# Scores and products with V side by side in two PSUM tiles, and batch 1's loads in the rooms of late weights

## The chip, the cores and the metric

The kernel runs on one NeuronCore of a Trainium2 chip. The metric is the device time of one execution in microseconds (us). Below, TensorE is PE in the profile's rows, VectorE DVE, ScalarE ACT, GpSimd POOL and SyncE SP; PEld is TensorE's loading of weights beside its matmuls.

## The reference, cut to what matters

```
scores = scale * q @ k.T                       # 4 batches, 8 heads, 576 positions, 64 wide
heads 0-3: causal, the last 32 positions       # "local"
heads 4-7: causal, same position modulo 32     # "strided"
attn = exp(scores - max) / (sum + 1e-9);  x = attn @ v            # -> 2304 tokens x 512
h = relu(x @ w_in);  x = (s*h*h + b) @ w_out                      # 512 -> 2048 -> 512
# then: 8 experts; a token goes on if x @ w_skip > 0, to its best expert by x @ w_gate
out = x;  out[sel] = x + gate * (relu(x @ w1[e]) @ w2[e])         # 512 -> 1024 -> 512
```

All of it is float32. Attention is computed only where the masks leave something.

## The kernel before, in words

The work of a token passes through three parts: attention, a dense layer of 2048 hidden units (called MoE below, as in the code), and the experts.

**Attention.** There are 16 pairs of heads, four for each batch, in the order local, strided, local, strided (`HPS`); pair n has batch n // 4. Each pair has three units (`add_unit`, line 313), so there are twelve units for each batch. A unit computes scores by matmuls (line 341) into the PSUM tile `sc`, the maximum over each row on VectorE (L349), exponentials with their sums on ScalarE (L359), the reciprocal and the product with it on VectorE (L368), a transposition on TensorE into the PSUM tile `pt` (L373), a copy to SBUF (`moved`, L377, recorded at L234), the product with V on TensorE into the PSUM tile `xo` (L390), and two copies into the MoE's input `xb`: a rounded part (L395, recorded at L234 or L236) and the rest by a subtraction on VectorE (L397). In pairs 0 to 7 the mask is added by a matmul (L336), and ScalarE reads the scores from PSUM; in later pairs VectorE adds the mask (L345) and so reads `sc` once.

**MoE.** The tokens are in six blocks of 384. For each block and each of 16 slices of 128 hidden units there is a stage: twelve matmuls (L1028) with a slice of `w_in`, activation on ScalarE and VectorE, nine matmuls (L1071) with a slice of `w_out`. `SEGS` orders the stages: block 0 with slices 0 to 7, block 1 with all, block 0 with the rest, then blocks 2 to 5. Stage 8 is thus the first of block 1, whose tokens belong to batches 0 and 1, and stage 16 is the first that wants slice 8 of the weights. Each slice of a weight comes as 64-bit numbers by DMA (L481) and is converted on ScalarE and VectorE (L488 to L504). The first eight stages begin with three dummy matmuls each (L1024), and batch 0's units with four (L334).

**The order of the work.** All tasks are given to a planner (`Plan`, line 71), with estimated durations, a priority (the lower goes first), predecessors and rooms. It goes through the time, always gives the ready task with the best priority to a free engine, and writes down the order; the engines then work through it in that order, each on its own queue, and wait for each other by semaphores that the framework sets. A room (`Buf`) is a tag of a tile: a task that takes it waits until the last user of one of its tags is done. `sc`, `pt` and `xo` are one PSUM tile each, a bank of 512 columns; batch 0 may also use `h` for scores and the three `x2p` for `pt` and `xo`, since the MoE doesn't need them yet. A unit's priority is `FIRST[b] + STEP[b] * k`, k being its place in the batch; its tasks on TensorE come before every MoE stage (-5000), those on the other engines compete with the conversion of weights, whose priority is the number of the stage. Units of batches 2 and 3 also wait for the stage that has their priority's number (`gates`, line 1166).

**Loads.** SyncE issues them in the planner's order. V of batch 0's four pairs has a room for each pair, in the tiles `wi8` to `wi11` and `wo8` to `wo11` that weights fill later (`V_ROOM`, line 254); V of all later pairs has the one tile `vl`, and its load waits for the pair before to finish its products (L307). Queries and keys lie in `qkl` (local) and `qks` (strided), one tile each, refilled after the scores of the pair that used it last (L303); those of pairs 0, 2 and 3 have rooms in the tiles of late weights (`QK_ROOM`, line 255).

**Routing.** After a block's last stage its rows are turned, and the logits of the gate are gathered over some 20 us in the tile `sc` (`add_routing`, line 545, L599).

Of the kernel before, what the change touches and what calls it, by code (L numbers as in the profile page):

```python
# [20 lines left out]
BLK = 384  # L21
# [12 lines left out]
FIRST = (-1000.0, 0.0, 26.0, 48.0)  # L34
STEP = (1.2, 0.6, 1.8, 1.3)
LATE, LEAD = 3.0, 0
# [15 lines left out]
CLS = [3 * t for t in range(10)] + [29]  # L52
NOWHERE = 4096

CAPS = {"s_": 2, "gh": 2, "gl": 2, "row": 3, "sm": 4, "h": 2}
# [98 lines left out]
def kernel(  # L154
# [49 lines left out]
    xb = [wp.tile([128, 2, 4, BLK], F32R, name=f"xb{i}") for i in range(3)]  # L204

    plan = Plan(CAPS)
    pools = {"s_": sp, "pts": sp, "r": sp, "sm": sp, "gh": gp, "gl": gp, "row": rp, "lo": rp, "h": ph, "sc": pm, "pt": pm, "xo": pm}

    def make(b, shape, dt):
        tag = b.tag  # L210
        pool = pools.get(tag) or (px if tag.startswith("x2p") else wp)
        return pool.tile(shape, dt, name=tag, bufs=CAPS.get(tag, 1))
# [8 lines left out]
    def c_a(n, psum=False):  # L221
        return {"A": (0.13 if psum else 0.16) + n / 1400}
# [4 lines left out]
    def c_dma(n):  # L227
        return {"SP": max(0.06, n / 360e3)}
# [24 lines left out]

    V_ROOM = {n: (f"wi{8 + n}", f"wo{8 + n}") for n in range(4)}
    QK_ROOM = {0: ("wi12", "wo12"), 2: ("wi13", "wo13"), 3: ("wi14", "wo7")}

    def add_pair(n):
# [22 lines left out]
        def load_v(e):  # L280
            if b == 0:
                for h in range(2):
                    vt[h] = make(vbuf[h], [nk, nt_all, D], F32)
                    SY.dma_start(vt[h][:], vd[:, h])
            else:
                v = vb[0:nk, 0:2 * nt_all * D].rearrange("p (h t d) -> p h t d", h=2, t=nt_all)
                SY.dma_start(v, vd)
                vt[:] = [v[:, 0], v[:, 1]]
# [12 lines left out]
        else:  # L301
            last = last_qk.get(loc)
            lq = [plan.add(c_dma(512 * src.shape[1]), load_qk, p0 - 4, after=s_tasks[last] if last is not None else (), lat=DMA)] * 2  # L303
            last_qk[loc] = n
        if b == 0:
            vbuf = [Buf([r]) for r in V_ROOM[n]]
        lv = plan.add(c_dma(4 * nk * 2 * nt_all * D), load_v, p0 - 3.5, after=o_tasks.get(n - 1, ()) if b else (), take=vbuf, lat=DMA)  # L307
        s_tasks[n], o_tasks[n] = [], []
# [4 lines left out]
    def add_unit(n, b, hp, g, loc, qk, vt, vbuf, qbuf, nq, nk, by_pe, prio, lq, lv):  # L313
# [3 lines left out]
        first = b == 0  # L317
        sc_b = Buf(["sc", "h"] if first else ["sc"])
        s_b = Buf(["s_", "gh"] if first else ["s_"])
        pt_b = Buf(["pt", "x2p0"] if first else ["pt"])  # L320
        pts_b = Buf(["pts", "gl"] if first else ["pts"])
        xo_b = Buf(["xo", "x2p1", "x2p2"] if first else ["xo"])
        sm_b = Buf(["sm"])
# [7 lines left out]
        def scores(e):  # L331
            d["sc"] = sc = make(sc_b, [128, 512], F32)
            for _ in range(KEEP_S if first else 0):
                PE.matmul(sc[:, 288:512], one, msk[:, 0:224], start=True, stop=True)  # L334
            if by_pe:
# [209 lines left out]
    def add_routing(blk, last, xbuf, paused=None, near=None):  # L545
        P = -8000 + blk
        d = rt[blk] = {"rows": {}, "lg": sp.tile([128, 3, 9], F32, name="lg")}
        lp_b, ls_b, lt_b = Buf(["sc"]), Buf(["lo"]), Buf(["pt"])
        row_b = [Buf(["row"]) for t in range(3)]
# [29 lines left out]
        for k in range(4):  # L579
# [15 lines left out]
            def logit(e, k=k):  # L595
                if k == 0:
                    d["lp"] = make(lp_b, [128, 512], F32)
                for m, x in ((18, d["xh"]), (9, d["xl"]))[::-1 if k == 3 else 1]:
                    PE.matmul(d["lp"][0:m, 0:BLK], wgr[:, k, 0:m], x[:], start=k == 0 and m == 18, stop=k == 3 and m == 18)  # L599

            a = plan.add(c_pe(128, 3, False), tr, P, after=cps + trs[:1], take=[pt_b] + ([] if trs else [lp_b]), use=row_b)
            trs.append(a)
            a = plan.add({**c_a(BLK, True), **c_v(BLK)}, xt_hi, P, after=[a], take=[hi_b], use=[pt_b])
            a = plan.add(c_v(BLK), xt_lo, P, after=[a], take=[lo_b], use=[pt_b, hi_b])
            lm = plan.add(c_pe(BLK, 2, False), logit, P, after=[a, lm, gate_w], use=[hi_b, lo_b, lp_b])

# [11 lines left out]

        a = plan.add({**c_a(BLK, True), **c_v(BLK)}, lg_row, P, after=[lm], take=[ls_b], use=[lp_b])
        a = plan.add({"PE": 0.35}, lg_turn, P, after=[a], take=[lt_b], use=[ls_b])  # L620
        lgs = [plan.add(c_v(54), lg_sum, P, after=[a], use=[lt_b])]
        sc_b = Buf(["sc"])
        a = plan.add({"V": 0.5}, lambda e: route_a(blk), P, after=lgs + [r_prev[0]])
# [161 lines left out]
    def turn():  # L785
        for t in range(4):
            if t < 3:
                pt = pm.tile([128, 4, 128], F32, name=("pt", "sc", "xo")[t])
            else:
                pt = ph.tile([128, 4, 128], F32, name="h")  # L790
            turn_in(pt, t)
            turn_hi(pt, t)
            turn_lo(pt, t)
# [62 lines left out]
    def last_x2(fill):  # L856
# [20 lines left out]
        for t in range(3):  # L877
            pt = pm.tile([128, 512], F32, name=("pt", "xo", "sc")[t])
            for k in range(4):
# [6 lines left out]
        ls = sp.tile([128, BLK], F32, name="r", bufs=1)  # L886
        lt = pm.tile([128, 512], F32, name="xo")
        for t in range(3):
# [14 lines left out]
    def experts():  # L903
# [17 lines left out]
        fill(3)  # L921
        rk, cn = (pm.tile([128, 512], F32, name=n_) for n_ in ("sc", "xo"))
        route_rank(NBLK - 1, rk)
# [172 lines left out]

    cn_b, ltp_b = Buf(["xo"]), Buf(["s_"])
    P, late = -7000, {}
# [161 lines left out]
```

## Time and profile before

| | us |
|---|---|
| three runs | 764.76, 763.86, 767.2 (median 764.76) |
| profiled execution | 763.24 |
| its span, first to last instruction | 761.4 |
| TensorE busy | 734.9 (97%) |
| VectorE busy | 375.4 (49%) |
| ScalarE busy | 296.0 (39%) |
| GpSimd busy | 62.7 (8%) |
| mean granted TensorE clock | 0.99 |

The profile is of one execution. Its times count from the first instruction. The page gives shares of the whole span; what belongs to one part of it is read from the views by stretch. A wait is put down to the engine that the semaphore came from last. A busy TensorE isn't TensorE at its peak, because matmuls overlap and their ends are modelled.

### The profile page before, as it was taken

How to read it: one execution, taken by the hardware profiler on the slowest of the kernel's cores; microseconds unless marked ns; L12 is line 12 of the kernel's file. 1: busy time of each engine (PE TensorE's matmuls, PEld its weight loads, DVE VectorE, ACT ScalarE, POOL GpSimd, SP SyncE). 2: the span in 40 equal slices, each digit the busy share in tenths (PEclk: the TensorE clock that was granted, in tenths of full speed). 3: DMA queues.
4: the chain of work that ended last, by engine and by line, in shares of the span. 5: the costliest groups of instructions: out<-in, count | busy, mean ns of one | idle time of the engine just before them, and what ended most of it. 6: DMA issues, size and time to landing. Idle time of an engine off the chain costs nothing.

```text
span 761.4 us, 11904 instructions
## 1 busy us (share of the span) xinstructions
PE 734.9 (97%) x4410; PEld 633.1 (83%) x4411; DVE 375.4 (49%) x1009; ACT 296.0 (39%) x813; POOL 62.7 (8%) x67
## 2 busy tenths in 40 slices
PE   9899989999999999999999999999999999999992
PEld 6788779998888888888888999898787888888791
DVE  4899999624565644456554324654442222313120
ACT  4787766424343543445453223533301402112020
POOL 0000000000010100010001002010032212011121
PEclk9999999999999999999999999999999999999997
DMA  9676685102231222012020005320214502011130
GB/s 294 221 208 207 201 280 142 51 0 84 76 113 48 71 65 80 27 48 78 27 84 1 2 1 174 107 80 5 79 36 142 220 37 75 14 42 56 43 72 32
DMA packets 23505, 69.00 MB, mean 91 GB/s; under 512 B 5035, under 2 KB 5291, under 8 KB 23430
## 3 DMA queue, kind: packets, MB, share of 16 engines
q1 hardware_dynamic: 19350, 56.81, 22.7%
q0 software_dynamic: 3936, 11.03, 4.7%
q8 instruction: 41, 0.67, 0.4%
q14 instruction: 34, 0.28, 0.1%
q10 hardware_dynamic: 144, 0.22, 0.1%
HBM read 52.94 MB, written 15.11 MB: 89 GB/s over the span
## 4 chain that ended last, share of the span: by engine, by line
PE 85%; DMA 5%; DVE 4%; issue 4%; ACT 1%; POOL 0%; POOLq 0%; DVEq 0%; ACTq 0%
PE h L1028 26%; PE x2p L1071 25%; PE h L801 10%; PE x2p L814 9%; DMA out<-row,ids 5%; PE sc L341 3%; PE xo L390 2%; PE pt L373 2%; PE sc L599 1%; PE pt L585 1%; PE h L1180 1%; PE h L341 1%; PE x2p L864 1%; PE h L1024 1%; DVE row L494 0%
## 5 line engine op out<-in xcount | busy, mean ns | idle before, releaser
L1028 PE MATMUL h<-xb,wi 128*128 128x384 f32 x1152 | 225.1, 344 | 2.0 <-ACT wi L234 1.2
L1028 PEld LDWEIGHTS h<-xb,wi 128*128 128x128 f32 x1152 | 203.9, 189 | 8.1 <-ACT wi L234 1.7
L1071 PE MATMUL x2p<-wo,gh 128*128 128x512 f32 x564 | 194.6, 399 | 0.0
L1071 PEld LDWEIGHTS x2p<-wo,gh 128*128 128x128 f32 x564 | 106.1, 188 | 20.1
L1071 PE MATMUL x2p<-wo,gl 128*128 128x512 f32 x282 | 111.1, 394 | 0.6 <-DVE gl L1061 0.4
L801 PE MATMUL h<-xb,wi 128*128 128x512 f32 (+1 forms) x480 | 103.3, 374 | 2.3 <-DVE row L818 1.8
L801 PEld LDWEIGHTS h<-xb,wi 128*128 128x128 f32 x480 | 83.4, 188 | 20.6 <-issue 2.8
L814 PE MATMUL x2p<-wi,wo 128*128 128x512 f32 x432 | 99.4, 390 | 0.0
L1036 DVE SCALAR_TENSOR_TENSOR r<-r,sbc 128x384 f32<-128x384 f32 x88 | 54.3, 617 | 85.7 <-ACT r L1033 85.6
L814 PEld LDWEIGHTS x2p<-wi,wo 128*128 128x128 f32 x432 | 80.8, 188 | 16.6
L1033 ACT ACTIVATE r<-h 128x384 f32<-128x384 f32 x96 | 47.0, 489 | 116.5 <-PE h L1028 111.2
L1040 ACT ACTIVATE gh<-r,sbc 128x384 fp32r<-128x384 f32 x88 | 54.3, 617 | 77.5 <-PE x2p L1071 53.6
L1045 DVE SCALAR_TENSOR_TENSOR gl<-r,sbc,gh 128x384 fp32r<-128x384 f32 x88 | 54.3, 617 | 59.1 <-ACT gh L1040 57.8
L804 ACT ACTIVATE wo<-h 128x512 fp32r<-128x512 f32 (+1 forms) x40 | 22.2, 554 | 144.0 <-PE h L801 139.1
L805 DVE SCALAR_TENSOR_TENSOR wo<-h,wo 128x512 fp32r<-128x512 f32 (+1 forms) x40 | 25.5, 638 | 76.5 <-ACT wo L804 72.3
L1071 PEld LDWEIGHTS x2p<-wo,gl 128*128 128x128 f32 x282 | 53.1, 188 | 9.4 <-DVE gl L1061 0.7
L703 POOL DMA_INDIRECT lst<-pay,ii x18 | 18.4, 1020 | 466.1 <-DVE ii L697 444.9
L818 DVE SCALAR_TENSOR_TENSOR row<-x2p,ids,xb 128x512 f32<-128x512 f32 x14 | 10.5, 751 | 61.8 <-PE x2p L814 61.8
L390 PEld LDWEIGHTS xo<-pts,vl 96*64 96x64 f32 (+1 forms) x480 | 16.9, 135 | 12.5 <-issue 4.5
L390 PE MATMUL xo<-pts,vl 96*64 96x64 f32 (+1 forms) x480 | 21.6, 226 | 3.6 <-DVE xb L397 2.1
L819 POOL DMA_INDIRECT out<-row,ids x14 | 13.9, 995 | 107.5 <-DVE row L818 93.2
L397 DVE TENSOR_TENSOR xb<-xo,xb 128x192 fp32r<-128x192 f32 (+4 forms) x59 | 18.3, 336 | 5.8 <-ACT xb L234 5.6
(479 smaller groups left out, 769.1 us busy)
## 6 DMA issues: line engine op xcount, KB each, us to landing
wo<-in_w SPq DMA_DIRECT2D x16, 512.0 KB, 5.8
qks<-in_qkstr SPq DMA_DIRECT2D x7, 882.0 KB, 6.5
wo<-in_w_out SPq DMA_DIRECT2D x12, 512.0 KB, 3.7
x2d<-row SPq DMA_DIRECT2D x21, 256.0 KB, 3.9
qkl<-in_qkloc SPq DMA_DIRECT2D x6, 864.0 KB
wo<-in_w_in SPq DMA_DIRECT2D x10, 512.0 KB, 4.0
out<-row SPq DMA_DIRECT2D x18, 256.0 KB, 2.0
wi<-in_w_in SPq DMA_DIRECT2D x6, 512.0 KB
```

The source lines that it names most:

```text
L341: PE.matmul(sc[0:nq, i * nk:(i + 1) * nk], qt, qk[0][:, k0:k0 + nk], start=not by_pe, stop=not by_pe or i == nt - 1)
L390: PE.matmul(xo[64 * h:64 * h + 64, c:c + m], vt[h][:, t, :], d["pts"][0:nk, r:r + m], start=True, stop=True)
L801: PE.matmul(p[:, 0:N], W[f][:, w, k * 128:(k + 1) * 128], x[:, k, 0:N], start=n == 0, stop=n == 11)
L804: A.activation(h[:, 0, 0:N], p[:, 0:N], AF.Relu)
L805: V.scalar_tensor_tensor(h[:, 1, 0:N], p[:, 0:N], 0.0, h[:, 0, 0:N].bitcast(F32), op0=ALU.max, op1=ALU.subtract)
L814: PE.matmul(y[:], K["h"][f][:, g, c], W[NFE + f][:, w, :], start=n == 0, stop=n == 3 * NFE - 1)
L1028: PE.matmul(p[:, 0:BLK], win_t[fc][:, w, k * 128:(k + 1) * 128], x[:, k, :], start=n == 0, stop=n == 11)
L1033: A.activation(d["r"][:], d["p"][:, 0:BLK], AF.Relu)
L1036: V.scalar_tensor_tensor(d["r"][:], d["r"][:], sbc[:, 0:1], d["r"][:], op0=ALU.mult, op1=ALU.mult)
L1040: A.activation(gh[:], d["r"][:], AF.Identity, bias=sbc[:, 1:2])
L1045: V.scalar_tensor_tensor(gl[:], d["r"][:], sbc[:, 1:2], gt[i][0][:].bitcast(F32), op0=ALU.add, op1=ALU.subtract)
L1071: PE.matmul(x2p[t][:], g[:, c], wout_t[fc][:, w, :], start=begins and n == 0, stop=ends and n == 2)
```

## The change

- The tiles `sc` and `xo` are replaced by two tiles `sx0` and `sx1` of one bank each. Of each, columns 0 to 287 are a room for scores (`sc0`, `sc1`) and columns 288 to 511 one for products with V (`xo0`, `xo1`). The number of PSUM banks stays at eight. A unit takes whichever score room and whichever product room the planner has free first.
- Routing takes `sc0` and `xo0` together for its logits, which are 384 columns wide.
- V of batch 1's four pairs gets the rooms `wi8` to `wi11` and `wo8` to `wo11` too, after batch 0's; its load no longer waits for the pair before.
- Queries and keys of pairs 6 and 7 get rooms in `wi12`, `wo12`, `wi13` and `wo13`, after those of pairs 0 and 2. `qkl` and `qks` then pass from pairs 4 and 5 to pairs 8 and 9.
- `STEP` of batch 1 goes from 0.6 to 0.3, so its units have priorities 0 to 3.3 instead of 0 to 6.6, and its loads come correspondingly earlier.
- The dummy matmuls of batch 0's units write columns 0 to 223 in place of 288 to 511.

```diff
-STEP = (1.2, 0.6, 1.8, 1.3)
+STEP = (1.2, 0.3, 1.8, 1.3)
...
+SCW = 288
...
+    sx = [pm.tile([128, 512], F32, name=f"sx{i}") for i in range(2)]
+    halves = {f"sc{i}": sx[i][:, 0:SCW] for i in range(2)} | {f"xo{i}": sx[i][:, SCW:512] for i in range(2)}
...
         tag = b.tag
+        if tag in halves:
+            return halves[tag]
...
-    V_ROOM = {n: (f"wi{8 + n}", f"wo{8 + n}") for n in range(4)}
-    QK_ROOM = {0: ("wi12", "wo12"), 2: ("wi13", "wo13"), 3: ("wi14", "wo7")}
+    V_ROOM = {n: (f"wi{8 + n % 4}", f"wo{8 + n % 4}") for n in range(8)}
+    QK_ROOM = {0: ("wi12", "wo12"), 2: ("wi13", "wo13"), 3: ("wi14", "wo7"), 6: ("wi12", "wo12"), 7: ("wi13", "wo13")}
...
         def load_v(e):
-            if b == 0:
+            if n in V_ROOM:
...
-        lv = plan.add(c_dma(4 * nk * 2 * nt_all * D), load_v, p0 - 3.5, after=o_tasks.get(n - 1, ()) if b else (), take=vbuf, lat=DMA)
+        lv = plan.add(c_dma(4 * nk * 2 * nt_all * D), load_v, p0 - 3.5, after=() if n in V_ROOM else o_tasks.get(n - 1, ()), take=vbuf, lat=DMA)
...
-        sc_b = Buf(["sc", "h"] if first else ["sc"])
+        sc_b = Buf(["sc0", "sc1"] + ["h"] * first)
...
-        xo_b = Buf(["xo", "x2p1", "x2p2"] if first else ["xo"])
+        xo_b = Buf(["xo0", "xo1"] + ["x2p1", "x2p2"] * first)
...
-                PE.matmul(sc[:, 288:512], one, msk[:, 0:224], start=True, stop=True)
+                PE.matmul(sc[:, 0:224], one, msk[:, 0:224], start=True, stop=True)
...
-        lp_b, ls_b, lt_b = Buf(["sc"]), Buf(["lo"]), Buf(["pt"])
+        lp_b, ls_b, lt_b = [Buf(["sc0"]), Buf(["xo0"])], Buf(["lo"]), Buf(["pt"])
...
-                    d["lp"] = make(lp_b, [128, 512], F32)
+                    d["lp"] = sx[0]
```

The rest of the diff passes the new names on (routing's other tasks, the count of tokens, and the experts' part, where the tiles are used whole).

## Rows read from the trace of the kernel before

**Rows 1.** The page, part 1: busy us of each engine (share of span), instructions.
```profile
PE 734.9 (97%) x4410; PEld 633.1 (83%) x4411; DVE 375.4 (49%) x1009; ACT 296.0 (39%) x813; POOL 62.7 (8%) x67
```

**Rows 2.** Table of stretches: length, busy us by engine (instructions), clock, DMA share, GB/s.
```profile
core 0: us, PE busy (x) PEld busy (x) DVE busy (x) ACT busy (x) POOL busy (x), PEclk, DMA share, GB/s
7.35:33.90 26.55, 25.92 (x342) 24.29 (x341) 20.08 (x89) 20.60 (x104) 0.00 (x0) 1.00 0.85 286
33.90:41.00 7.10, 5.12 (x22) 4.13 (x21) 7.10 (x22) 3.20 (x15) 0.00 (x0) 0.76 0.52 148
36.50:40.70 4.20, 3.41 (x12) 3.36 (x13) 4.20 (x13) 1.60 (x7) 0.00 (x0) 0.59 0.74 227
41.00:92.90 51.90, 50.92 (x397) 42.54 (x396) 48.53 (x129) 40.71 (x130) 0.00 (x0) 1.00 0.67 213
92.90:103.20 10.30, 6.02 (x73) 4.65 (x71) 10.23 (x29) 7.62 (x26) 0.00 (x0) 1.00 0.77 269
30.00:103.20 73.20, 65.47 (x550) 54.27 (x546) 69.33 (x192) 55.31 (x179) 0.00 (x0) 0.98 0.63 204
...
110.50:170.00 59.50, 59.50 (x299) 53.99 (x299) 39.93 (x72) 27.98 (x51) 0.00 (x0) 1.00 0.25 75
170.00:410.00 240.00, 239.78 (x1590) 210.30 (x1589) 126.82 (x396) 104.08 (x320) 9.31 (x9) 1.00 0.19 64
```

**Rows 3.** Waits, 92.9 to 103.3 us: who for whom, us, times, longest.
```profile
PE xo L390 <- DVE xb L397: 2.1, 1, 2.1
...
PE pt L373 <- DVE sm L352: 0.8, 1, 0.8
PE xo L390 <- ACT pts L234: 0.7, 1, 0.7
PE sc L336 <- ACT s__1369 L359: 0.7, 1, 0.7
```

**Rows 4.** Timeline of SyncE's queue: start, us, engine, line, transfer.
```profile
19.94 0.33 SPq L481 DMA_DIRECT2D wi<-in_w_in  x1
...
69.34 0.33 SPq L287 DMA_DIRECT2D vl<-in_vloc  x1
...
89.92 0.30 SPq L287 DMA_DIRECT2D vl<-in_vstr  x1
```

**Rows 5.** Chain of waits, 92.9 to 103.3 us: start, us, what.
```profile
93.58 0.60 DVE row L497
94.18 0.60 DVE row L494
...
99.76 0.60 DVE wi L504
100.36 0.60 DVE wo L504
100.96 0.34 DVE lo L491
```

**Rows 6.** Stretches, line 504 alone (last step of a conversion): VectorE's busy us, instructions.
```profile
30.00:103.20 73.20, 12.94 (x19) 0.98 0.63 204
```

**Rows 7.** Timeline of TensorE, 33 to 49 us: start, us, what, [idle before].
```profile
35.87 0.62 PE L1028 MATMUL h<-xb,wi 128*128 128x384 f32 x2 [1.18 <-ACT wi L234]
37.29 3.40 PE L1028 MATMUL h<-xb,wi 128*128 128x384 f32 x10 [0.80 <-DVE wi L504]
...
40.98 0.80 PE L341 MATMUL sc<-qkl 128*128 128x96 f32 x6
```

**Rows 8.** The page, part 6: loads of local queries and keys, KB each.
```profile
qkl<-in_qkloc SPq DMA_DIRECT2D x6, 864.0 KB
```

**Rows 9.** Timeline of VectorE, 100.9 to 102.6 us.
```profile
101.21 0.27 DVE L236 CAST xb<-xo 128x72 fp32r<-128x72 f32 x1
```

**Rows 10.** Timeline of ScalarE, 100.5 to 102.4 us.
```profile
101.52 0.40 ACT L234 CAST xb<-xo 128x144 fp32r<-128x144 f32 x1 [0.21 <-DVE xb L236]
```

**Rows 11.** Stretch of one unit's exponentials (line 359 alone): ScalarE's busy us, instructions.
```profile
92.35:93.61 1.26, 1.26 (x8) 1.00 0.42 114
```

More of the change, by code (lines that the diff above doesn't have):

```diff
@@ L204 @@
     xb = [wp.tile([128, 2, 4, BLK], F32R, name=f"xb{i}") for i in range(3)]
+    sx = [pm.tile([128, 512], F32, name=f"sx{i}") for i in range(2)]
+    halves = {f"sc{i}": sx[i][:, 0:SCW] for i in range(2)} | {f"xo{i}": sx[i][:, SCW:512] for i in range(2)}
     plan = Plan(CAPS)
-    pools = {"s_": sp, "pts": sp, "r": sp, "sm": sp, "gh": gp, "gl": gp, "row": rp, "lo": rp, "h": ph, "sc": pm, "pt": pm, "xo": pm}
+    pools = {"s_": sp, "pts": sp, "r": sp, "sm": sp, "gh": gp, "gl": gp, "row": rp, "lo": rp, "h": ph, "pt": pm}
     def make(b, shape, dt):
         tag = b.tag
+        if tag in halves:
+            return halves[tag]
         pool = pools.get(tag) or (px if tag.startswith("x2p") else wp)
@@ L304, in add_pair @@
             last_qk[loc] = n
-        if b == 0:
+        if n in V_ROOM:
             vbuf = [Buf([r]) for r in V_ROOM[n]]
-        lv = plan.add(c_dma(4 * nk * 2 * nt_all * D), load_v, p0 - 3.5, after=o_tasks.get(n - 1, ()) if b else (), take=vbuf, lat=DMA)
+        lv = plan.add(c_dma(4 * nk * 2 * nt_all * D), load_v, p0 - 3.5, after=() if n in V_ROOM else o_tasks.get(n - 1, ()), take=vbuf, lat=DMA)
         s_tasks[n], o_tasks[n] = [], []
@@ L596, in logit @@
                 if k == 0:
-                    d["lp"] = make(lp_b, [128, 512], F32)
+                    d["lp"] = sx[0]
                 for m, x in ((18, d["xh"]), (9, d["xl"]))[::-1 if k == 3 else 1]:
                     PE.matmul(d["lp"][0:m, 0:BLK], wgr[:, k, 0:m], x[:], start=k == 0 and m == 18, stop=k == 3 and m == 18)
-            a = plan.add(c_pe(128, 3, False), tr, P, after=cps + trs[:1], take=[pt_b] + ([] if trs else [lp_b]), use=row_b)
+            a = plan.add(c_pe(128, 3, False), tr, P, after=cps + trs[:1], take=[pt_b] + ([] if trs else lp_b), use=row_b)
             trs.append(a)
@@ L604, in add_routing @@
             a = plan.add(c_v(BLK), xt_lo, P, after=[a], take=[lo_b], use=[pt_b, hi_b])
-            lm = plan.add(c_pe(BLK, 2, False), logit, P, after=[a, lm, gate_w], use=[hi_b, lo_b, lp_b])
+            lm = plan.add(c_pe(BLK, 2, False), logit, P, after=[a, lm, gate_w], use=[hi_b, lo_b, *lp_b])
         def lg_row(e):
@@ L617, in lg_sum @@
             V.tensor_reduce(d["lg"][:], d["lt"][:, 0:54].rearrange("p (t h e) -> p t e h", t=3, h=2), axis=AX.X, op=ALU.add)
-        a = plan.add({**c_a(BLK, True), **c_v(BLK)}, lg_row, P, after=[lm], take=[ls_b], use=[lp_b])
+        a = plan.add({**c_a(BLK, True), **c_v(BLK)}, lg_row, P, after=[lm], take=[ls_b], use=lp_b)
         a = plan.add({"PE": 0.35}, lg_turn, P, after=[a], take=[lt_b], use=[ls_b])
         lgs = [plan.add(c_v(54), lg_sum, P, after=[a], use=[lt_b])]
-        sc_b = Buf(["sc"])
+        sc_b = Buf(["sc0", "sc1"])
         a = plan.add({"V": 0.5}, lambda e: route_a(blk), P, after=lgs + [r_prev[0]])
@@ L787, in turn @@
             if t < 3:
-                pt = pm.tile([128, 4, 128], F32, name=("pt", "sc", "xo")[t])
+                pt = pm.tile([128, 4, 128], F32, name=("pt", "sx0", "sx1")[t])
             else:
@@ L877, in last_x2 @@
         for t in range(3):
-            pt = pm.tile([128, 512], F32, name=("pt", "xo", "sc")[t])
+            pt = pm.tile([128, 512], F32, name=("pt", "sx1", "sx0")[t])
             for k in range(4):
@@ L886, in last_x2 @@
         ls = sp.tile([128, BLK], F32, name="r", bufs=1)
-        lt = pm.tile([128, 512], F32, name="xo")
+        lt = pm.tile([128, 512], F32, name="sx1")
         for t in range(3):
@@ L921, in experts @@
         fill(3)
-        rk, cn = (pm.tile([128, 512], F32, name=n_) for n_ in ("sc", "xo"))
+        rk, cn = (pm.tile([128, 512], F32, name=n_) for n_ in ("sx0", "sx1"))
         route_rank(NBLK - 1, rk)
@@ L1094 @@
                 add_routing(blk, t, xbuf, pause.get(blk), mm1s[-6] if blk in pause else None)
-    cn_b, ltp_b = Buf(["xo"]), Buf(["s_"])
+    cn_b, ltp_b = Buf(["xo0", "xo1"]), Buf(["s_"])
     P, late = -7000, {}
```

## The prediction

> **What bounds the kernel now.** I read the page's busy shares first: TensorE is busy for 734.9 of 761.4 us, VectorE for half of that [rows 1]. So time can only come out of TensorE's idle time, its work, or its clock. The change leaves TensorE's work as it is (the same matmuls of the same widths), so I looked next at a table of stretches for where the idle time lies [rows 2]. The reader is to see four things in it. From 110.5 to 410 us, where the units of batches 2 and 3 run among the MoE stages, TensorE idles 0.22 of 299.5 us: nothing to win there, though something to lose. In batch 0's stretch (7.35 to 33.9) it idles 0.6. From 33.9 to 103.2 it idles 1.98 + 0.98 + 4.28 = 7.24 us. And in that last part VectorE is the engine that never rests: 7.10 of 7.10, 48.53 of 51.90, 10.23 of 10.30 us. After it the staging of weights goes on, but TensorE waits for nothing more.
>
> Third view: the waits in 92.9 to 103.2 [rows 3]. All four of TensorE's waits are in the last units of batch 1, the three of pair 7: its second product with V for VectorE's subtraction out of the one product tile (2.1), its transposition for VectorE's maximum step (0.8), its first product for ScalarE's copy (0.7), its scores for the exponentials that read the one score tile (0.7). Fourth, SyncE's queue [rows 4]: V of pairs 6 and 7 is issued at 69.34 and 89.92, because the single V buffer has to be read out first; pair 7 thus starts its transpositions at the earliest some us after 89.92, when TensorE has already begun stage 7. Stage 8, the first of block 1, needs every strided unit of batch 1, so TensorE runs dry. Fifth, the chain of waits in this stretch [rows 5]: it lies on VectorE, and half of it is the conversion of weights in steps of 0.34, 0.60, 0.60 and 0.60 us, between which the short steps of pair 7 stand in line.
>
> **The change part by part.** The profiled execution took 763.24 us: a span of 761.4 and 1.84 around it. The median of the three runs shown, 764.76, lies 1.52 above. I make the sum on 763.24 and add 1.52.
>
> *The end of batch 1.* Three edits have one answer. With its own V rooms, pair 7's V no longer waits for pair 6's last product. With two score tiles and two product tiles, two of the four waits of [rows 3] lose their cause. With a step of 0.3 instead of 0.6 the twelve units have priorities 0 to 3.3 instead of 0 to 6.6, so that on VectorE they pass the conversions of stages 4 and up. Can VectorE supply this? One conversion is 0.34 + 3 x 0.60 = 2.14 us [rows 5]; nineteen were finished between 30 and 103.2 [rows 6], but stage 8 needs only fifteen (w_in of stages 0 to 7, w_out of 0 to 6). Deferring four takes 8.6 off VectorE's 69.33 us [rows 2], leaving 60.8; at its present share of 0.947 that is 64.2 us. TensorE's own work in the stretch is 65.5 [rows 2]. The two are level, and both are under 73.2, so the 4.28 us may go. What is deferred isn't missed: from 110.5 to 170 VectorE has 59.5 - 39.9 = 19.6 us free [rows 2] for 8.6. Bounds: 0 (the wait only moves to the weights) to -4.3. I take -4.3, because the named waits are this stretch's whole idle time.
>
> *The front, 33.9 to 41.* Stage 0 starts at 35.87 after 1.18 us of waiting for its first weights, and waits 0.80 more after two matmuls [rows 7]. Pair 4's third score group, 0.80 us, runs only at 40.98, behind them, because the second unit holds the score tile. With two tiles it can move into this gap: -0.8. Against this, both halves of pair 6's queries and keys (864 KB [rows 8]) now go into rooms of pair 0, free early, at priority -2.2 and -1.95; they pass the constants and the first weight, which was issued at 19.94 [rows 4] into queues that were 0.85 busy at 286 GB/s [rows 2]. 864 KB at that rate is 3.0 us of later weights. I cost it at nothing, since VectorE and TensorE have batch 0's and pair 4's units to do until 33.9; if that cover is gone the price is 3.0. [...] I take -0.8, nearest to the one piece of work whose row shows that it can move.
>
> *The shared banks.* Scores and products now lie side by side in one tile, so in one bank. The planner keeps them as separate rooms; what the chip waits for is decided by the bank. [Rows 9, 10] show it: for one product tile VectorE reads 72 columns from 101.21 for 0.27 us, and ScalarE, which reads other columns, starts at 101.52, after 0.21 us idle that is put down to VectorE. So a product with V can have to wait for the exponentials of a later unit whose scores lie beside it, and scores for the subtractions of an earlier one. An instruction that so waits at TensorE's head holds the MoE matmuls behind it. One unit's four exponentials take 1.26 us [rows 11]. Bounds: 0 (a wait that is added gains nothing) to 12 units of batch 1 x 1.26 = 15.1. I take +1.0: three units at 0.35, half of the 0.7 that the score tile costs once now [rows 3]. The low end is nearer, since between a unit's scores and its product there mostly lie blocks of 9 or 12 matmuls, and in batches 2 and 3 the score half is read once by VectorE and is free.
>
> [...]
>
> *What costs nothing.* V of four pairs goes in two loads each, and queries and keys of pairs 6 and 7 too: six more issues at 0.33 us on SyncE's queue [rows 4], beside SyncE's long waits. The moved loads of batch 2 (its first scores now follow pair 4's and 5's) come earlier into a queue that the later stages leave idle. Their rooms belong to weights needed from stage 16, long after batch 1. The four dummy matmuls per unit of batch 0 only change columns. Routing now takes both halves of a tile, some 20 us at a time, and units then have one tile: hidden by MoE matmuls, which fill 239.78 of 240 us [rows 2]; without that cover a unit's 0.7.
>
> Sum: 763.24 - 4.3 - 0.8 + 1.0 = 759.1, and with 1.52: **760.7 us**, 0.5% under the median.
>
> **The rivals.**
> *The wait moves to the weights (20%).* Passed by twelve units, the conversions of stages 1 to 7 come late, and TensorE waits in front of those stages for what it saved in front of stage 8. For it: VectorE is as good as full from 33.9 on [rows 2], and TensorE already waited 1.18 + 0.80 for weights once [rows 7]. Against it: the four conversions that can be deferred. 764.76 - 0.8 + 1.0 = 765.0.
> *The shared bank decides (14%), slower.* Place: products of batch 1, whose exponentials run late because ScalarE and VectorE are behind; the unit two later has the same tile by turns and starts its exponentials just when this one's transposition gives back their output buffer. At two thirds of 1.26, 0.84 for twelve units: 10.1. 764.76 - 5.1 + 10.1 = 769.8. It decides from (5.1 + 3.8) / 12 = 0.74 us a unit. For it: [rows 9, 10]; against: one such wait on the score tile in the stretch, of 0.7 [rows 3], where it was single.
> *Everything goes (10%).* All of 7.24, and the clock's 1.4: 764.76 - 8.6 = 756.1. For it: the level sums of TensorE and VectorE. [...]
> *The loads don't come earlier where it counts (8%).* SyncE's queue is in order; pair 6's load of 864 KB stands ahead of the first weight and its 3.0 us reach TensorE: 760.7 + 3.0 = 763.7.
>
> **How the numbers follow.** The forecast has 48%, with a range of its own of 758.7 to 762.2. A measurement of this kernel can tell about 0.5% (3.8 us) from no change; its three runs lie 3.3 us apart. Faster by more, under 760.9: 0.30 of the forecast's 0.48 and the 0.10 of "everything": 0.40. Within: 0.18 + 0.20 + 0.08 = 0.46. Slower: 0.14. The range 757.0 to 768.0 leaves out most of the bank's case and the better half of "everything".
>
> **What would show it.** Right: in the profile after, V of pair 7 is issued before 60 us; TensorE's idle time between 41 and the start of stage 8 falls from 5.3 to about 2; stage 8 starts near 98 instead of 103; VectorE's nineteenth conversion ends after stage 8 has begun. Wrong in the first step: TensorE's waits for VectorE's weights grow by as much as those of batch 1 shrink. Wrong in the third: waits of scores or products for exponentials or subtractions of another unit over 2 us in sum, or idle time after 110 us that wasn't there. The front is wrong if stage 0 starts after 38. I'd be wrong altogether if the time went anywhere behind 170 us, where I cost everything at nothing.

## The result and the profile after

The changed kernel takes 768.82 us (median of 9 runs, 767.59 to 770.32), the kernel before 763.98 in the 9 runs beside them: a ratio of 1.0055, 95% interval 1.0042 to 1.0068. It is slower by 4.2 us by the ratio (4.8 between the medians), where 760.7 was predicted and the range ended at 768.0. The profiled execution has a span of 767.1 us against 761.4, 5.7 more. The two profiles overstate the usual distance a little: the mean granted clock of the changed kernel's nine runs is 0.982 or 0.983; that of the kernel before was 0.990 in its profiled execution, but 0.987 in about half of its runs beside the experiments.

First the page of the changed kernel, part 1 (line numbers of the kernel after are higher by 8 from the attention units on: L398 is the product with V, L349 the scores, L344 the mask's matmul, L367 the exponentials, L242 and L244 copies, L405 the subtraction, L489 the weight loads):

```profile
PE 739.3 (96%) x4410; PEld 637.3 (83%) x4411; DVE 374.4 (49%) x1002; ACT 298.1 (39%) x820; POOL 62.5 (8%) x67
```

Against [rows 1] the same 4410 matmuls take 4.4 us more of TensorE's time, and its idle time grows by only 1.3 (767.1 - 739.3 = 27.8 against 26.5). So most of the 5.7 us is not waiting but work at the lower clock (the mean granted clock from 30 to 103.2 is 0.88 below, 0.98 in [rows 2]). The stretches of the same kernel, with the columns of [rows 2], say where:

```profile
33.90:41.00 7.10, 2.63 (x21) 2.41 (x22) 4.44 (x17) 4.80 (x22) 0.00 (x0) 0.68 0.92 333
41.00:46.00 5.00, 5.00 (x30) 4.06 (x30) 5.00 (x16) 2.54 (x10) 0.00 (x0) 0.50 0.68 217
...
53.00:58.00 5.00, 4.95 (x27) 3.92 (x28) 4.59 (x17) 3.83 (x14) 0.00 (x0) 0.66 0.75 264
...
41.00:92.90 51.90, 47.50 (x389) 39.94 (x389) 43.59 (x132) 36.20 (x127) 0.00 (x0) 0.89 0.51 157
92.90:103.20 10.30, 10.30 (x59) 8.34 (x58) 8.18 (x17) 6.35 (x15) 0.00 (x0) 0.92 0.68 193
30.00:103.20 73.20, 64.27 (x531) 54.06 (x530) 59.04 (x177) 49.25 (x172) 0.00 (x0) 0.88 0.59 185
110.50:170.00 59.50, 59.22 (x298) 53.52 (x297) 48.23 (x88) 32.89 (x60) 0.00 (x0) 1.00 0.40 127
170.00:410.00 240.00, 240.00 (x1586) 210.66 (x1586) 125.29 (x378) 105.57 (x325) 9.01 (x9) 1.00 0.19 64
```

The 4.28 us of idle time at 92.9 to 103.2 are gone (10.30 of 10.30 busy), as forecast, but stage 8 starts at 107.2, near 98 by the forecast and at 103.2 before. And 33.9 to 41 idles 4.47 instead of 1.98, 41 to 92.9 idles 4.40 instead of 0.98, and there the mean granted clock is 0.89 instead of 1.00: at 41 to 46 it is 0.50, at 53 to 58 it is 0.66. VectorE, 69.33 of 73.20 us busy before, is at 59.04: it waits too. From 110.5 to 410 nothing is lost: 0.28 us of idle time at full clock. TensorE's waits in the changed kernel:

```profile
PE sx L398 <- ACT s__629 L367: 3.1, 1, 3.1
PE sx L398 <- ACT pts L242: 2.7, 2, 1.9
PE sx L344 <- DVE xb L244: 1.8, 1, 1.8
PE sx L344 <- ACT s__654 L367: 1.4, 1, 1.4
```

The first and the third are across the two halves of a tile: a product waits for the exponentials of another unit, scores wait for the copy of another unit's product. They and the fourth are the gaps that stand before the stretches at clocks of 0.50 and 0.66 (TensorE's timeline, idle time in brackets):

```profile
36.96 0.35 PE L398 MATMUL sx<-gl,wi 54*64 54x54 f32 x1 [3.11 <-ACT s__629 L367]
...
37.97 1.44 PE L349 MATMUL sx<-qkl 128*128 128x96 f32 x6
40.81 0.34 PE L344 MATMUL sx<-im 108*108 108x216 bf16 x1 [1.41 <-ACT s__654 L367]
...
44.87 1.52 PE L1036 MATMUL h<-xb,wi 128*128 128x384 f32 x3
...
53.05 0.23 PE L344 MATMUL sx<-im 108*108 108x162 bf16 x1 [1.75 <-DVE xb L244]
```

Stage 0 starts at 44.87 instead of 35.87 [rows 7], far past the 38 that was named as the sign of a wrong front. SyncE's queue shows one reason:

```profile
17.01 0.33 SPq L281 DMA_DIRECT2D wi<-in_qkloc  x1
26.01 0.33 SPq L292 DMA_DIRECT2D wi<-in_vloc  x1
26.43 0.37 SPq L292 DMA_DIRECT2D wo<-in_vloc  x1
26.95 0.48 SPq L292 DMA_DIRECT2D wi<-in_vstr  x1
...
29.66 0.43 SPq L489 DMA_DIRECT2D wi<-in_w_in  x1
```

SyncE's own waits in the first 60 us:

```profile
SPq L292 <- PE sx L398: 17.0, 3, 8.3
```

V of pair 4 goes into pair 0's room, and its load stands at the head of the queue until TensorE has done pair 0's products (the 8.3 us; it is issued at 26.01). Behind it are V of pair 5, the constants and the first weight: issued at 29.66 instead of 19.94 [rows 4]. ScalarE, in turn, has the conversion of that weight at its head, ahead of a unit's copies and exponentials (ScalarE's timeline):

```profile
34.23 0.66 ACT L496 ACTIVATE lo<-wi 128x512 f32<-128x512 f32 x1 [2.29 <-DMA wi<-in_w_in]
...
36.48 0.33 ACT L367 ACTIVATE s__629<-sx,sm 128x96 f32<-128x96 f32 x1
36.71 0.20 ACT L367 ACTIVATION_READ_ACCUMULATOR s__629<-sx,sm 128x1 f32 x1
...
39.44 0.40 ACT L242 CAST xb<-sx 128x96 fp32r<-128x96 f32 x2 [1.97 <-PE sx L349]
```

The last line is the other reason. This cast reads a finished product out of columns 288 and up; its matmuls ended at 37.8. It starts 1.6 us after that, when the scores (L349) that TensorE has begun meanwhile are done. The profile doesn't number the two tiles; that these scores stand beside the product in the same tile is concluded from the versions with whole tiles below, where no copy waits so. ScalarE's waits, and below them VectorE's, from 33 to 103 us, give the sum:

```profile
ACT xb L242 <- PE sx L349: 6.6, 4, 2.7
```

```profile
DVE xb L405 <- ACT xb L242: 7.1, 3, 3.9
...
DVE xb L244 <- PE sx L349: 1.4, 2, 0.9
```

A copy out of one half waits for the next unit's scores in the other, four times (6.6 us), and VectorE's subtraction behind it on its queue for up to 3.9 us. By these waits two rooms of columns were one room for the engines. Each of these tiles is one bank, so the rows don't tell whether a wait goes by the tile or by the bank. They are waits for semaphores that the framework sets; what the chip would do with two accesses at once, no run here shows.

### The profile page after: what moved, and what is told of

Its sections match the earlier page's. It is cut to its first block, busy times and chain, and to the rows that moved or that the text cites. A ratio compares the mean times of both kernels' runs of the same rounds, so it can differ in the third digit from the quotient of the medians.

```text
span 767.1 us, 11888 instructions
## 1 busy us (share of the span) xinstructions
PE 739.3 (96%) x4410; PEld 637.3 (83%) x4411; DVE 374.4 (49%) x1002; ACT 298.1 (39%) x820; POOL 62.5 (8%) x67
## 4 chain that ended last, share of the span: by engine, by line
PE 85%; DMA 6%; issue 4%; ACT 1%; DVE 1%; SPq 0%; POOL 0%; POOLq 0%; ACTq 0%
PE h L1036 26%; PE x2p L1079 25%; PE h L809 10%; PE x2p L822 8%; DMA out<-row,ids 5%; PE sx L349 4%; PE sx L398 3%; PE pt L381 2%; PE sx L607 1%; PE pt L593 1%; PE h L1188 1%; PE h L1032 1%; DMA x2d<-row 1%; DMA wi<-in_w_in 1%; PE x2p L872 1%
## 5 line engine op out<-in xcount | busy, mean ns | idle before, releaser
L809 PE MATMUL h<-xb,wi 128*128 128x512 f32 (+1 forms) x480 | 103.3, 374 | 2.2 <-DVE row L826 1.0
L405 DVE TENSOR_TENSOR xb<-sx,xb 128x192 fp32r<-128x192 f32 (+4 forms) x62 | 18.9, 335 | 17.6 <-ACT xb L242 16.2
L242 ACT CAST xb<-sx 128x192 fp32r<-128x192 f32 (+4 forms) x44 | 12.5, 331 | 28.2 <-PE sx L349 14.0
L827 POOL DMA_INDIRECT out<-row,ids x14 | 13.9, 996 | 107.2 <-DVE row L826 93.2
L242 ACT COPY pts<-pt 96x384 f32<-96x384 f32 (+2 forms) x37 | 17.7, 479 | 7.6 <-PE pt L381 7.5
```

Source lines behind the costliest of these rows:

```text
L242: A.copy(dst, src)
L809: PE.matmul(p[:, 0:N], W[f][:, w, k * 128:(k + 1) * 128], x[:, k, 0:N], start=n == 0, stop=n == 11)
```

## The experiments

The theories: Q, SyncE's queue (the moved loads hold up the weights); B, the shared banks; S, the step of 0.3. A ratio is to the kernel before on the same chip, with its 95% interval. Two more explanations stand behind them: that VectorE bounds the stretch whatever the buffers, or that V's single buffer does, on which the forecast stood.

**Queue and banks, two by two.** The changed kernel with V of pairs 4 to 7 and the early queries and keys issued by GpSimd:

```diff
-                    SY.dma_start(vt[h][:], vd[:, h])
+                    (G if b else SY).dma_start(vt[h][:], vd[:, h])
...
-            SY.dma_start(qk[h][:], src[:, c])
+            (G if b else SY).dma_start(qk[h][:], src[:, c])
```

> The changed kernel, but the loads that wait for batch 0's rooms (V of pairs 4 to 7, queries and keys of pairs 6 and 7) are issued from GpSimd's queue, which has nothing else to do there; order, rooms and tiles stay. Theory Q (SyncE's queue): V of pair 4 stands at the head of SyncE's queue from 17.3 to 26.0 us, waiting for the last product of pair 0, and the first weight behind it is issued at 29.66 in place of 19.94; all else follows from it. Then this kernel takes 759 to 764 us, the first weight is issued near 20, stage 0 starts before 38. Theory B (shared banks): TensorE's waits for the other half of a tile (3.1 for exponentials, 1.8 for a copy) and the low clock after them are the loss. Then it stays at 767 to 770 us.

Measured 767.4 us, 1.0045 [1.0032, 1.0057]. The waits across the halves stay, but the first shrinks: the product that had waited 3.1 us waits 1.4.

```profile
PE sx L344 <- DVE xb L244: 1.8, 1, 1.8
PE sx L344 <- ACT s__654 L367: 1.4, 1, 1.4
PE sx L398 <- ACT s__629 L367: 1.4, 1, 1.4
```

So by this comparison some 1.7 of the 3.1 us were the late first weight passed on through ScalarE, and not the bank. That is how two causes can hide in one row: the wait is put down to the exponentials, and these had waited for a DMA. Stage 0 still starts at 42.2, though the first weight is now issued at 21.34.

The same with both tiles as whole rooms (a tile holds scores or a product, never both):

```diff
-    halves = {f"sc{i}": sx[i][:, 0:SCW] for i in range(2)} | {f"xo{i}": sx[i][:, SCW:512] for i in range(2)}
+    halves = {f"sx{i}": sx[i] for i in range(2)}
...
-        sc_b = Buf(["sc0", "sc1"] + ["h"] * first)
+        sc_b = Buf(["sx0", "sx1"] + ["h"] * first)
...
-        xo_b = Buf(["xo0", "xo1"] + ["x2p1", "x2p2"] * first)
+        xo_b = Buf(["sx0", "sx1"] + ["x2p1", "x2p2"] * first)
```

> The whole change with both suspects taken away: GpSimd's queue for the loads that wait for batch 0's rooms, and each of the two tiles one room. Theories Q and B together: 764 us or less, 4 to 6 below the changed kernel. Theory S: 766 or more.

Measured 765.64 us, 1.0011 [0.9996, 1.0025], between the two times that were expected. And whole tiles with SyncE's queue, the last edit alone on the changed kernel:

> The changed kernel with each of the two tiles as one room (scores or products, never both), all loads on SyncE's queue as in the change. It is the missing corner of four: with GpSimd's queue the shared tile cost 2.6 us (1.0045 against 1.0011). If the two causes add, this one gives after's 1.0055 less 0.0034 = 1.002 (765.6 us). If SyncE's queue alone is enough to lose the front (V of pair 4 waits at its head for 8 us, first weight issued near 29 us, stage 0 after 43 us), it stays at 1.004 to 1.0055. Waits of a product or of scores for another unit's exponentials or copies beside it: none in either case.

Measured 766.51 us, 1.0027 [1.0009, 1.0045]; the first weight is issued at 29.06 us, as late as in the changed kernel, and in neither kernel with whole tiles does a copy wait for scores. The four: 1.0055 and 1.0027 with SyncE's queue, 1.0045 and 1.0011 with GpSimd's. Whole tiles are worth 0.28% and 0.34%, 2.1 and 2.6 us; the queue alone 0.10% and 0.16%, 0.8 and 1.2 us, which is less than the intervals resolve. GpSimd's queue takes the waiting load out of the weights' way but not its bytes (in the first experiment the DMA share from 7.35 to 33.9 is 1.02 at 319 GB/s, in [rows 2] 0.85 at 286). With it and whole tiles the first weight is issued at 21.03 us, and ScalarE starts its conversion at 32.21 without having waited for it, but stage 0 is as late as this:

```profile
32.21 0.71 ACT L496 ACTIVATE lo<-wi 128x512 f32<-128x512 f32 x1
```

```profile
40.32 2.78 PE L1036 MATMUL h<-xb,wi 128*128 128x384 f32 x12
```

So the wait at the head of the queue is only a part of the late front.

**The order of the loads.** Whole tiles, SyncE's queue, V of pair 4 back in its own buffer, and the early loads of pairs 5 to 7 planned later:

```diff
-    V_ROOM = {n: (f"wi{8 + n % 4}", f"wo{8 + n % 4}") for n in range(8)}
+    V_ROOM = {n: (f"wi{8 + n % 4}", f"wo{8 + n % 4}") for n in (0, 1, 2, 3, 5, 6, 7)}
...
-                lq.append(plan.add(cost, fn, p0 - 4 + h / 4, take=[qbuf[h]], lat=DMA))
+                lq.append(plan.add(cost, fn, p0 - 4 + h / 4 + 4 * (n in (6, 7)), take=[qbuf[h]], lat=DMA))
...
-load_v, p0 - 3.5, after=() if n in V_ROOM else
+load_v, p0 - 3.5 + 4 * (n in (5, 6, 7)), after=() if n in V_ROOM or n == 4 else
```

> The changed kernel with whole tiles, SyncE's queue, V of pair 4 in its own free buffer, and the early loads of pairs 5 to 7 planned four stages later, so that the first three weights are issued ahead of them. Theory that the loads ahead of the first weights are what is left of the loss (1.0027 with them): first weight issued near 20 us, stage 0 near 36 to 37 us, ratio 0.997 to 1.000. Theory that the rest is lost elsewhere, at VectorE: 1.001 to 1.003.

Measured 764.62 us, 1.0001 [0.9982, 1.002]. SyncE's queue in it:

```profile
15.39 0.32 SPq L295 DMA_DIRECT2D vl<-in_vloc  x1
...
20.98 0.33 SPq L489 DMA_DIRECT2D wi<-in_w_in  x1
...
28.62 0.30 SPq L292 DMA_DIRECT2D wi<-in_vstr  x1
...
29.52 0.35 SPq L281 DMA_DIRECT2D wi<-in_qkloc  x1
```

The first weight is back at 20.98, stage 0 at 36.3, and no loss is left that the interval shows. From 1.0055 by 1.0027 to 1.0001: 2.1 us for the banks, 2.0 for the order of the loads, together the whole 4.2. The last step by itself is at the edge of its interval; both together are far outside. The edit moves the waiting load, the bytes and the start of batch 1's units at once; which of them gives the 2.0, these runs don't tell.

This kernel has the parts of the change without the shared banks and the late front (pair 4's V is back in its own buffer), and so is the fairest test of the gain that was forecast. Its stretches:

```profile
41.00:92.90 51.90, 51.90 (x404) 43.80 (x404) 49.38 (x142) 40.76 (x139) 0.00 (x0) 0.97 0.60 191
92.90:103.20 10.30, 8.85 (x74) 6.66 (x73) 10.00 (x27) 8.21 (x23) 0.00 (x0) 0.83 0.43 118
```

TensorE idles 1.45 us in them, against 5.26 in [rows 2]; 2 was forecast. Yet stage 8 starts at 103.1. In this execution the granted clock is 0.97 and 0.83 there and was 1.00 before: an estimate from these rows is 51.90 x 0.03 + 8.85 x 0.17 = 3.1 us of the 3.8 that the waits gave back. From 110.5 to 170 TensorE idles 1.84 us, where it idled nothing before.

**Parts of the change on the kernel before.** The tiles side by side alone (loads and step as before):

```diff
+    sx = [pm.tile([128, 512], F32, name=f"sx{i}") for i in range(2)]
+    halves = {f"sc{i}": sx[i][:, 0:SCW] for i in range(2)} | {f"xo{i}": sx[i][:, SCW:512] for i in range(2)}
```

> The kernel before with the two shared tiles alone: loads and STEP 0.6 as before. Theory Q: first weight issued near 20, 762 to 764.5 us. Theory B: 767 to 769 us, with waits of scores or products for another unit's readers of over 2 us in sum.

Measured 767.45 us, 1.0047 [1.0032, 1.0062]. The step alone:

```diff
-STEP = (1.2, 0.6, 1.8, 1.3)
+STEP = (1.2, 0.3, 1.8, 1.3)
```

> The kernel before with STEP of batch 1 at 0.3 and nothing else. Theory S (step): the units pass the conversions of the first weights on VectorE, so stages 1 to 3 come late whatever the loads and tiles do: 765.5 to 768 us, stage 1 after 46. If queue and banks were all of it (theories Q and B): 763 to 764.5 us.

Measured 765.53 us, 1.0015 [1.0004, 1.0027]. Rooms for V, queries and keys with the step of 0.3, on the two single tiles `sc` and `xo`:

```diff
-STEP = (1.2, 0.6, 1.8, 1.3)
+STEP = (1.2, 0.3, 1.8, 1.3)
...
+    V_ROOM = {n: (f"wi{8 + n % 4}", f"wo{8 + n % 4}") for n in range(8)}
+    QK_ROOM = {0: ("wi12", "wo12"), 2: ("wi13", "wo13"), 3: ("wi14", "wo7"), 6: ("wi12", "wo12"), 7: ("wi13", "wo13")}
```

> The kernel before with the change's loads and step alone: V rooms for pairs 4 to 7, rooms for queries and keys of pairs 6 and 7, STEP 0.3; scores and products keep their one tile each. Theory Q: the queue is as in the changed kernel, so 767 to 770 us, first weight issued after 26. Theory B: no shared bank, so 764 us or less.

Measured 766.81 us, 1.0037 [1.0024, 1.0051], just under theory Q's range, with the first weight at 25.75. The same with GpSimd's queue (the edit of the first experiment):

> All of the change but the shared tiles, with the loads that wait for batch 0's rooms on GpSimd's queue: neither the shared banks nor SyncE's queue can hold TensorE. Theories Q and B together: 764 us or less, since what is left are earlier loads and a closer step. Theory S, or the earlier loads taking the DMA engines from the first weights: 765.5 to 767.5.

Measured 765.58 us, 1.0016 [0.9998, 1.0033]: here the queue is worth 0.21%, at the edge of what the intervals resolve. Each part alone makes the kernel slower, and the parts do not add (0.47% for the tiles and 0.37% for the rest, against 0.55% for all).

V of pair 4 alone in pair 0's room, the rest as before:

```diff
-    V_ROOM = {n: (f"wi{8 + n}", f"wo{8 + n}") for n in range(4)}
+    V_ROOM = {n: (f"wi{8 + n % 4}", f"wo{8 + n % 4}") for n in range(5)}
```

> The kernel before with one load moved: V of pair 4 goes into pair 0's room, and nothing else is changed. Theory Q: this load alone holds the queue for the last product of pair 0, the first weight is issued some 5 to 9 us later than 19.94, 765 to 769 us. Theory B: 764 us.

Measured 770.26 us, 1.0079 [1.005, 1.0109], above theory Q's range, and mostly not for its reason: the first weight is issued 3.9 us later (23.82), stage 0 starts at 37.4, and the loss lies at the end of batch 1, where scores wait 3.4 us for exponentials and stage 8 starts at 107.9 instead of 103.2. Why this one room moves the end of the batch so much was not tried further.

Whole tiles alone (tiles `sx0` and `sx1`, each one room as above), with the loads and the step of before:

> As the run with the two tiles alone, but each of the two tiles is one room that takes scores or products, not both side by side, so that the planner counts every wait that the chip makes. Loads and step as before. Theory B (waits between the halves that the planner doesn't count): 762.5 to 764.5 us, where the side-by-side tiles alone took 767.45, and no wait of TensorE over 1 us for another unit's readers. If any new order of the units costs as much: 766.5 or more.

Measured 773.09 us, 1.0122 [1.0095, 1.0149], where a gain was hoped for. TensorE's waits:

```profile
PE sx L398 <- DMA vl<-in_vstr: 5.8, 1, 5.8
```

With two tiles the units come faster than the single V buffer is refilled. So the tiles need the V rooms; with V of pairs 6 and 7 in rooms, issued by GpSimd,

```diff
+    V_ROOM = {n: (f"wi{8 + n % 4}", f"wo{8 + n % 4}") for n in (0, 1, 2, 3, 6, 7)}
```

> Two whole tiles for scores and products, step 0.6, queries and keys as before; only V of pairs 6 and 7 gets rooms in late weights, issued by GpSimd. The version that keeps what helped (the front of the kernel with whole tiles, whose loss at 57 us was 7.5 against 8.9 before) and takes away what hurt there (5.8 us of waiting for pair 7's V). Theory that the end of batch 1 is bound by V's buffer: 0.994 to 0.998 (759.5 to 762.5 us), stage 8 near 99 us. Theory that VectorE, full from 34 to 103 us, bounds the stretch whatever the buffers: 0.999 to 1.002, stage 8 at 102 to 104 us, the wait for V turned into waits for VectorE.

it took 765.82 us, 1.0022 [1.0007, 1.0037]: that wait is gone, and 1.0% with it, but stage 8 starts at 104.8, where a limit by V's buffer asked for 99. The whole-tile kernel on GpSimd's queue with the step back at 0.6:

```diff
-STEP = (1.2, 0.3, 1.8, 1.3)
+STEP = (1.2, 0.6, 1.8, 1.3)
```

> The changed kernel with whole-tile rooms, batch 1's loads on GpSimd's queue, and batch 1's step back at 0.6. Theory that what is left of the loss (1.0011 in the same kernel with 0.3) is the early loads and early units of batch 1 ahead of the first weights: 0.998 to 1.000, first conversion done near 36.5 us. Theory that the end of batch 1 needs the step of 0.3: 1.002 or more, with stage 8 starting after 103 us.

Measured 769.4 us, 1.0064 [1.0034, 1.0093] against 1.0011 with 0.3. The step was no mistake of the change: with two tiles and early V it is worth 0.5%.

**What bounds the end of batch 1.** V of pairs 6 and 7 in rooms, on the kernel before, single tiles, step 0.6 (the same `V_ROOM`):

> The kernel before, single tiles and step 0.6, with V of pairs 6 and 7 alone in rooms of late weights, issued by GpSimd. If V's buffer holds up the end of batch 1: 0.995 to 0.998. If the end is bound by VectorE or by the single score and product tiles: 0.999 to 1.002, with TensorE's waits of 4.3 us in the last units of batch 1 still there (for other rows).

Measured 767.86 us, 1.0035 [1.002, 1.0049], above both expectations. This tests V's late issue by itself, as far as an edit can: the planner's order and the issuing queue change with it. Pair 7's V is now issued at 33.71 us by GpSimd, not at 89.92 [rows 4]; pair 6's at 48.82:

```profile
33.71 0.74 POOL L284 DMA_DIRECT2D wi<-in_vstr  x1 [32.60 <-PE x2p L390]
...
48.82 0.60 POOL L284 DMA_DIRECT2D wi<-in_vloc  x1 [13.80 <-PE x2p L390]
```

And stage 8 starts at 107.1 instead of 103.2. (The profiled execution is the slowest of the ten, 770.15 us, and its granted clock is 0.88 from 92.9 to 103.2 and 0.50 from 103.2 to 110.5.) TensorE at the end of the batch:

```profile
100.35 0.59 PE L373 MATMUL pt<-im,s__1404 108*54 108x108 f32 x4 [1.78 <-DVE s__1404 L368]
103.84 0.35 PE L390 MATMUL xo<-pts,wi 54*64 54x54 f32 x1 [2.90 <-ACT pts L234]
```

Between the two stands ScalarE:

```profile
100.90 0.67 ACT L488 ACTIVATE lo<-wo 128x512 f32<-128x512 f32 x1 [1.33 <-DMA wo<-in_w_out]
101.48 0.29 ACT L359 ACTIVATE s__1466<-sc,sm 108x54 f32<-108x54 f32 x1
...
102.32 1.07 ACT L234 COPY row<-x2p 128x512 f32<-128x512 f32 x2
103.26 0.52 ACT L234 COPY pts<-pt 54x432 f32<-54x432 f32 x1
```

The transposition is over by 100.94. Its copy to SBUF (`pts`) starts 2.3 us later, behind a conversion's first step (0.67, for whose load ScalarE had waited 1.33 us), the exponentials of the last unit and two copies of a block's rows on ScalarE's queue. The wait of [rows 3] has only changed its name: what is late is the chain of short steps through ScalarE and VectorE, and at one point a weight's load, not V.

Next, how much of it is VectorE's load. One step of 0.60 us is left out of every weight's conversion (its low bits are then missing, and the output differs), in the kernel before, the changed one, and the one with whole tiles and GpSimd's queue:

```diff
         def low(e, d=d):
-            V.scalar_tensor_tensor(d["ci"], d["lw"], 29, d["ci"], op0=ALU.logical_shift_right, op1=ALU.bitwise_or)
+            pass
```

> The kernel before, with one of VectorE's 0.60 us steps left out of every weight's conversion (the low bits of the weights, so the output differs); the planned order is kept. Nineteen conversions run between 30 and 103 us, so VectorE has 11.4 us less to do there. Theory that VectorE, 95% busy in that stretch, bounds it: TensorE's 7.2 us of idle time there falls by at least 3, ratio 0.993 to 0.996. Theory that the order, the buffers or the loads bound it: 0.998 to 1.000.

> The changed kernel without the same 0.60 us step of VectorE. If what the change lost is VectorE's load alone, it comes level with the kernel before without that step. If the first weights' late issue (near 29 us) and the shared banks lose it, which don't depend on VectorE's load, it stays 0.004 to 0.006 above that kernel.

> The kernel with whole tiles and with batch 1's loads on GpSimd's queue, without the same step of VectorE. If the gain that was expected at the end of batch 1 (4.3 us) was absent because VectorE was full, it appears here: 0.003 to 0.006 under the kernel before without that step. If early V and two tiles give nothing in any case: within 0.002 of that kernel.

Measured 762.96, 769.41 and 762.17 us: 0.9982 [0.9968, 0.9997], 1.006 [1.0037, 1.0083] and 0.9967 [0.9954, 0.998]. VectorE's 11.4 us less are worth 1.4 us to the kernel before, which is under what the theory of a full VectorE asked for, and nothing to the changed one: its first weight still comes at 29.62, its product still waits 2.9 us. With whole tiles and GpSimd's queue they are worth 3.4 us (1.0011 to 0.9967), and that kernel then lies 0.15% under the kernel before without the step, which the intervals don't tell from nothing. So even with VectorE relieved, early V and a second tile give some 1 us by these runs, not 4.3; stage 0 starts at 39.6 there against 35.5, so a part may still be lost at the front.

Last, the same relief without leaving work out: the planner may give the conversion's last step to GpSimd, in the mended kernel and in the kernel before.

```diff
-        w_done[m, c] = [plan.add(c_v(512), rest, prio, after=[t], use=[c_b])]
+        w_done[m, c] = [plan.add({**c_v(512), **c_g(512)}, rest, prio, after=[t], use=[c_b])]
```

> The kernel with whole tiles and held loads, in which the planner may give the last step of a weight's conversion to GpSimd (1.29 us there, 0.60 on VectorE) when VectorE is busy. Taking one step of 0.60 us off VectorE was worth 3.4 us with whole tiles and early V (1.0011 to 0.9967). If VectorE's load holds that kernel: 0.996 to 0.998. If GpSimd's slower step makes the first weights late, or VectorE's load isn't what binds: 0.999 to 1.003.

> The kernel before with the same freedom for the last step of a conversion. Leaving a whole step out was worth 1.4 us there (0.9982), so at most 0.998; 0.999 to 1.002 if GpSimd's step is too slow. If the change's early loads and two tiles are worth something once VectorE is relieved, this one stays above the kernel with whole tiles and held loads by 0.001 to 0.003.

Measured 769.13 us, 1.0051 [1.0036, 1.0066], and 774.46 us, 1.0122 [1.0102, 1.0143]. Both theories missed. In the second, GpSimd's timeline and below it VectorE's:

```profile
98.69 1.27 POOL L504 TENSOR_TENSOR wo<-row,wo 128x512 fp32r<-128x512 f32 x1 [5.04 <-ACT wo L234]
```

```profile
98.95 1.55 DVE L494 SCALAR_TENSOR_TENSOR lo<-wo,lo 128x512 int32<-128x512 int32 x1
100.43 0.16 DVE L352 TENSOR_SCALAR sm<-sm 108x4 f32<-108x4 f32 x1
100.50 0.68 DVE L497 SCALAR_TENSOR_TENSOR row<-wo,row 128x512 int32<-128x512 int32 x1
```

A step of 0.68 takes 1.55 while GpSimd's runs, and from 30 to 103.2 us VectorE is busy for 70.49 us with 172 instructions, against 69.33 with 192 in [rows 2], though nine steps are moved away. No version here that leaves no work out beats the kernel before; the one with whole tiles and held loads beats the changed kernel by 0.54%.

## Why the prediction was wrong

**The end of batch 1 (-4.3).** The main step that fails. The stretch did lose its idle time, but because TensorE came into it late and still had stages in hand (stage 7 starts at 102.8 instead of 86.9, stage 8 at 107.2), not because the units were ready sooner. The prediction went from V that "no longer waits" to "the named waits are this stretch's whole idle time": it took V's late issue for a cause, and idle time for time. None of the four waits of [rows 3] is for V's load. With V 56 us earlier, in the run with that edit alone, stage 8 is later: the named waits were the ends of a chain that runs through two loaded engines, and taking away one end shows the next. With whole tiles and held loads the idle time from 41 to 103.2 does fall as forecast, from 5.26 to 1.45 us, but stage 8 starts at 103.1: some 3.1 us of what was won (the estimate above, from one execution) went into the lower clock. VectorE's balance held and decided nothing: from 30 us to stage 8 it was busy for 62.98 us, where 60.8 were forecast, fifteen conversions had then ended, as counted, and the nineteenth ended at 115.9. The first rival, that the wait moves to the weights, did not come as such: none of TensorE's four waits is for a weight.

**The front (-0.8).** Wrong, and the step that fails stands under "What costs nothing": the moved loads "beside SyncE's long waits". I counted their issues (six times 0.33 us) and their bytes, and did not ask whose room each load waits for. The 8% rival had the right place, but it counted only the bytes: a load at the head of the queue waits 8.3 us for TensorE, and behind the late weight is ScalarE's conversion with a unit's copies and exponentials behind that. The loads' order as a whole was measured at 2.0 us, that wait alone at 0.8 to 1.2, both at or under what the intervals resolve. How the rest divides between bytes and the order of the units is open.

**The shared banks (+1.0).** Direction and kind of wait right, size wrong: 2.1 and 2.6 us. The waits go across the planner's rooms, as it said: 3.1 and 1.8 us on TensorE, and, once each tile is one room, no copy that waits for scores; a tile and its bank are the same thing in all these kernels. The sum asked only which instruction at TensorE's head could wait, and named products and scores. The larger number is on the copying engines, 6.6 us on ScalarE and 7.1 behind it on VectorE, and comes back to TensorE later. The rival in which the bank decides (14%, 769.8) comes near the time by luck: it held the bank for the whole loss, at the products of batch 1; it is half, and the largest gaps are at the front.

**The clock.** It stood only in a rival's sum, as a gain that might come (1.4). That is an estimate from [rows 2], 3.41 busy us at a clock of 0.59 against 2.0 at 1.00, and no run of the change shows it: from 33.9 to 41 us the clock was 0.68 in the changed kernel and 0.77 with held loads, 0.76 before. Behind three gaps of 3.11, 1.41 and 1.75 us the granted clock was 0.50 and 0.66, and the same matmuls took 4.4 us more. A sum made of gaps alone thus misleads in both directions: of the 5.7 us lost here only 1.3 are idle time, and with held loads idle time that was won did not become time.

**Right:** pair 7's V before 60 us (issued at 37.84), nothing lost between 110.5 and 410 us, routing with both halves hidden by MoE matmuls.

What stays open: how the parts act on each other in the planned order. Also open is how much of the clock's part belongs to the profiled executions alone. Of thirteen versions that change only rooms, tiles, queues, the loads' order or the step, none is faster than the kernel before, and single edits of it cost from 0.15% to 1.2%, sometimes (V of pair 4) for reasons that were not followed up.

## What to carry to other kernels

Before a load is moved up, write down which earlier reader its room waits for and what stands behind it in the same queue: here one load at the head of a queue passed its wait of 8.3 us on to the first weight. Two rooms in one tile were here one buffer for the three engines that touched it (waits across the halves of up to 3.1 us on TensorE, 6.6 us in sum on ScalarE, 1.4 on VectorE), so ask for the copies out of it as well as for the matmuls into it. And test the cause of a wait before pricing its removal: take the named releaser away alone, as the early V did here, and see whether the next stage moves, and at which clock.

## What the hardware showed that was not expected

A GpSimd step cost VectorE more than it took off: in the kernel before with GpSimd allowed the last step, a VectorE step took 1.55 us instead of 0.68 beside a GpSimd step of 1.27 us that had taken 0.68 away. VectorE's step ends at 100.50, 0.54 us after GpSimd's (98.69 + 1.27 = 99.96). Not every step there is longer: one of the same line and size took 0.68 us from 59.87 on, within a GpSimd step of 2.49 us that starts at 59.23. GpSimd's own step, 1.27 us at 98.69, thus took up to 2.49 in the same kernel. Why the steps beside each other are sometimes longer, no run here shows.

In the changed kernel the granted clock fell in a gap of 3.11 us between TensorE's small matmuls (1.00 until 36.0) and was 0.50 from 36.5 to 46.7 us, with one more gap of 1.41; from 89 to 95 us it was 0.72, behind one gap of 1.87 us. The length of a gap alone does not tell when: in the kernel with held loads gaps of 0.85 us at most stand in 92.9 to 103.2, with a clock of 0.83, and in the kernel before one of 2.1 us [rows 3], with a clock of 1.00 [rows 2].
